# A list scheduler for the order of all engines, four score tiles in one visit and recurrence outputs by column tile, in a kernel that runs two attentions at once

## The chip, the cores and the metric

One core of one Trainium2 chip. The metric is the device time of one execution in microseconds (us), median of several. All profiled executions quoted here are fast; the page lists the clock that TensorE was granted, on average, beside the span.

TensorE multiplies matrices and writes PSUM (the pools of these kernels take 8 banks), VectorE and ScalarE copy and compute from PSUM into SBUF, GpSimd does small copies, and SyncE only issues transfers (its line in the trace is SPq). A transfer issued from an engine occupies that engine's queue for the time of the issue (a copy of V below: 0.50 us on GpSimd, 0.59 us on SyncE).

## The reference, cut to what matters

```python
def _A_ref(x, mem0, Wq, Wk, Wv, Wo, seg_len):      # S 2048, Dm 576, H 32, Dh 128, M 8, seg_len 32
    mem = mem0
    for s in range(n_seg):                          # 64 segments, one after the other
        h = concatenate([mem, x[s]], axis=1)        # 8 memory rows + 32 tokens = 40
        q, k, v = h @ Wq, h @ Wk, h @ Wv            # 32 heads of 128
        p = softmax(where(mask, q @ k.T * scale, -1e9))
        o = (p @ v) @ Wo
        mem = o[:, :M]; outs.append(o[:, M:])       # the memory of the next segment
    return concatenate(outs)

def _B_ref(x, wqkv, wo):                            # plain attention, 32 heads of 18
    ...
a = _A_ref(...); b = _B_ref(...); g = sigmoid((x * gate_w).sum(-1))
return g * a + (1 - g) * b
```

A is a recurrence: segment s+1 needs the outputs of segment s. B is independent of it and is used to fill the waits of A.

## The kernel before

Each segment is a chain: projections (tile pvv) evacuated to tm, transposes (pt), scores (psh), exponential, row sums (pss), their reciprocals spread by TensorE (prb), values (pso), outputs (acc), and a fold (pw) into ht, the input of the next segment. The queries, keys and values of tokens do not depend on the memory. Those of the last 8 tokens of each segment are projected ahead, 16 segments at a time (pv, vl); their outputs, which the memory doesn't need, are made four segments at a time (otl). B's score tiles are sb, exponentials etb, values ob. The order is the order of the program text, and a generator steps B forward at fixed places (`tick`). V reaches its place in v_sb by four small copies per half, issued on SyncE.

```python
def b_steps():
    ...
            for jp in range(2):
                sb = ps_bs.tile([P, 2, QC], FP32, name="sb")          # two buffers of two banks
                for i in range(2):
                    j = 2 * jp + i
                    nc.tensor.matmul(sb[:, i, :], lhsT=kc[32*j:32*j+32, o:o+P],
                                     rhs=qch[gq][32*j:32*j+32, :], ..., tile_position=(32 * j, 0))
                nc.scalar.activation(out=etb[:, :, :], in_=sb[:, :, :], func=ACT.Exp, scale=scale_b)
                ...
        def project(w, starts):
            pv = ps_a.tile([P, 512], FP32, name="pvv", tag="pb")
            ...
            tm = seg2.tile([P, 512], BF16, name="tm", bufs=4)
            nc.vector.tensor_copy(out=tm[:, :], in_=pv[:, :])
            tick()
            return tm
        ...
        def project_v(b):
            tm = project(wv, ...)
            for jj in range(2):
                for u in range(2):
                    nc.sync.dma_start(out=v_sb[...], in_=tm[64 * jj + 32 * u:64 * jj + 32 * u + CT, :])

        tq2 = [project(wq, ...) for hf in range(2)]
        tk2 = [project(wk, ...) for hf in range(2)]
        turn(tq2, qt)                       # transposes: the four tm are free after these
        turn(tk2, kt3)
        project_v(0)
        ...                                 # psh, exponential, minimum
        project_v(1)
        ...                                 # idle-filling matmuls when no last-token work is left
    def out_project(acc, o, t0, b, d0, d1):           # each column tile j: other heads, all columns d0..d1
        for i in range(4):
            for j in range(4):
                nc.tensor.matmul(acc[32*j:32*j+32, 0:d1-d0], lhsT=o[:, h, t0:t0+CT], rhs=wo[:, h, d0:d1], ...)
    # hl = high and low half of acc on VectorE; the fold adds the four partial sums by matmul
```

The softmax here doesn't subtract the row's maximum and nothing guards it: scores larger than these inputs give would overflow.

## Time and profile before

| part of the span | us |
|---|---|
| time, median of 3 runs | 2015.8 |
| start (to the first projection of segment 0) | 259.7 |
| 63 segment intervals, mean | 26.02 |
| end (from the start of the last segment) | 109.4 |

"Interval" is the time from one segment's first pvv matmul to the next one's, read from the trace. The table of engines by stretch, for the three parts (columns: stretch, its length, then busy us and instructions of TensorE, its weight loads, VectorE, ScalarE and GpSimd, mean granted clock, busy share of the DMA engines, GB/s):

```profile
0.00:259.70 259.70, 206.13 (x1376) 96.16 (x1380) 74.68 (x154) 112.98 (x157) 39.49 (x77) 0.87 0.60 177
259.70:1899.10 1639.40, 1589.73 (x24377) 822.09 (x24378) 892.78 (x2149) 924.45 (x1017) 135.21 (x331) 0.98 0.16 38
1899.10:2008.50 109.40, 84.33 (x822) 45.07 (x822) 52.40 (x115) 46.17 (x49) 0.40 (x1) 0.84 0.33 92
```

In the segments TensorE is busy 97% of the time at nearly full clock, which is why the argument is about TensorE's time there. One more row matters later, that of the values product, which reads v_sb (columns: busy us, mean ns | idle before, what ended it):

```profile
L713 PE MATMUL pso<-et,v_sb 64*128 64x40 bf16 x2048 | 63.5, 180 | 2.8 <-DVE et L705 2.6
```

TensorE lost 2.8 us in all before pso, 2.6 of them to the multiply of et; its weight loads waited 1.7 us for V copies, 4 times.

### The profile page before, as it was taken

How to read it: one execution, taken by the hardware profiler on the slowest of the kernel's cores; microseconds unless marked ns; L12 is line 12 of the kernel's file. 1: busy time of each engine (PE TensorE's matmuls, PEld its weight loads, DVE VectorE, ACT ScalarE, POOL GpSimd, SP SyncE). 2: the span in 40 equal slices, each digit the busy share in tenths (PEclk: the TensorE clock that was granted, in tenths of full speed). 3: DMA queues.
4: the chain of work that ended last, by engine and by line, in shares of the span. 5: the costliest groups of instructions: out<-in, count | busy, mean ns of one | idle time of the engine just before them, and what ended most of it. 6: DMA issues, size and time to landing. Idle time of an engine off the chain costs nothing.

```text
span 2008.5 us, 60909 instructions
## 1 busy us (share of the span) xinstructions
PE 1880.2 (94%) x26570; PEld 963.3 (48%) x26570; DVE 1019.9 (51%) x2416; ACT 1083.6 (54%) x1222; POOL 175.1 (9%) x409
## 2 busy tenths in 40 slices
PE   6599899999999999999999999999999999999968
PEld 3243444555554455555544555554444444444434
DVE  2043255555554555555555555545554555545535
ACT  2345555555554555555556555555554555555544
POOL 5000001000100001000010001100010000100000
PEclk9599999999988999999999999989998999999979
DMA  8742631121221112211111112210111011100042
GB/s 275 256 116 91 167 63 53 31 41 29 50 46 42 34 34 50 45 37 39 43 54 34 36 36 51 47 35 26 28 40 35 26 28 32 30 24 26 20 119 82
DMA packets 242479, 118.04 MB, mean 59 GB/s; under 512 B 166236, under 2 KB 234660, under 8 KB 240676
## 3 DMA queue, kind: packets, MB, share of 16 engines
q1 hardware_dynamic: 231440, 91.43, 18.0%
q0 software_dynamic: 6048, 16.52, 2.6%
q10 hardware_dynamic: 4724, 6.20, 1.1%
q8 instruction: 208, 3.41, 0.7%
q14 instruction: 59, 0.48, 0.1%
HBM read 59.42 MB, written 37.88 MB: 48 GB/s over the span
## 4 chain that ended last, share of the span: by engine, by line
PE 74%; DVE 6%; issue 3%; ACT 2%; DMA 1%; ACTq 0%; SPq 0%; DVEq 0%; POOL 0%
PE pvv L616 22%; PE sb L210 14%; PE acc L540 9%; PE ob L190 7%; PE psh L662 3%; PE pt L632 3%; PE pv L297 3%; PE prb L697 3%; PE pw L561 2%; ACT etb L219 2%; PE idle L470 2%; PE pso L713 2%; DVE ot L721 2%; PE po L783 2%; PE pv L285 2%
## 5 line engine op out<-in xcount | busy, mean ns | idle before, releaser
L219 ACT ACTIVATE etb<-sb 128x1024 bf16<-128x1024 f32 x1024 | 1028.6, 1025 | 820.0 <-PE sb L210 789.2
L210 PE MATMUL sb<-qch,kch 32*128 32x512 bf16 x2048 | 442.5, 395 | 18.6 <-ACT etb L219 12.6
L625 DVE CAST tm<-pvv 128x512 bf16<-128x512 f32 x384 | 265.0, 690 | 215.4 <-PE pvv L616 212.7
L616 PEld LDWEIGHTS <-ht 128*32 128x32 bf16 x7680 | 197.2, 97 | 202.9 <-issue 45.8
L190 PE MATMUL ob<-etb,vch 128*32 128x512 bf16 x2048 | 235.8, 399 | 24.8 <-ACT etb L219 16.0
L540 PE MATMUL acc<-wo,ot 128*32 128x384 bf16 (+1 forms) x4096 | 204.6, 299 | 9.7 <-DVE ot L721 3.2
L210 PEld LDWEIGHTS <-kch 32*128 32x128 bf16 x2048 | 105.0, 91 | 218.5 <-issue 195.1
L540 PEld LDWEIGHTS <-ot 128*32 128x32 bf16 x4096 | 116.5, 99 | 85.3 <-DVE ot L721 48.2
L616 PE MATMUL pvv<-wq_m,ht 128*32 128x512 bf16 x2048 | 138.2, 388 | 11.0 <-DVE ht L738 8.6
L616 PE MATMUL pvv<-wv_m,ht 128*32 128x512 bf16 x2048 | 143.4, 381 | 0.0
L721 DVE CAST ot<-pso 128x320 bf16<-128x320 f32 x256 | 113.5, 483 | 53.5 <-PE pso L713 53.5
L616 PE MATMUL pvv<-wk_m,ht 128*32 128x512 bf16 x2048 | 133.7, 380 | 0.0
L190 PEld LDWEIGHTS <-vch 128*32 128x32 bf16 x2048 | 68.4, 94 | 112.5 <-issue 88.6
L276 DVE CAST vl<-pv 128x512 bf16<-128x512 f32 x90 | 62.0, 690 | 106.2 <-PE pv L297 39.7
L705 DVE TENSOR_TENSOR et<-et,prb 128x320 bf16<-128x320 bf16 x128 | 62.3, 487 | 102.0 <-PE prb L697 101.9
L551 DVE CAST hl<-acc 128x384 bf16<-128x384 f32 (+1 forms) x160 | 72.4, 452 | 77.3 <-PE acc L540 76.6
L672 DVE TENSOR_TENSOR et<-et,cap 128x320 bf16<-128x320 bf16 x128 | 42.7, 337 | 103.3 <-ACT et L670 103.3
L608 POOL COPY qt<-xl 128x256 bf16<-128x256 bf16 x64 | 26.0, 406 | 656.4 <-issue 631.5
L662 PEld LDWEIGHTS <-kt 128*64 128x64 bf16 x2048 | 62.7, 111 | 34.3 <-issue 29.9
L662 PE MATMUL psh<-qt,kt 128*64 128x40 bf16 x2048 | 77.3, 189 | 0.0
L389 PE MATMUL pq<-xT,wpk 128*128 128x512 bf16 x320 | 76.8, 389 | 0.0
L552 DVE TENSOR_TENSOR hl<-acc,hl 128x384 bf16<-128x384 f32 (+1 forms) x160 | 72.9, 456 | 5.1
(118 smaller groups left out, 1913.1 us busy)
## 6 DMA issues: line engine op xcount, KB each, us to landing
v_sb<-tm SPq DMA_DIRECT2D x512, 32.0 KB
wo<-in_A_Wo_dram SPq DMA_DIRECT2D x4, 1152.0 KB
qtd<-stg SPq DMA_DIRECT2D x32, 128.0 KB
wv_m<-in_A_Wv_dram SPq DMA_DIRECT2D x4, 1024.0 KB
qch<-qtd POOLq DMA_DIRECT2D x32, 128.0 KB, 2.5
ktd<-stg SPq DMA_DIRECT2D x32, 128.0 KB
wq_m<-in_A_Wq_dram SPq DMA_DIRECT2D x4, 1024.0 KB
vgd<-vt SPq DMA_DIRECT2D x32, 128.0 KB
```

What stands on the lines that cost most here:

```text
L190: mm = nc.tensor.matmul(ob[32 * j:32 * j + 32, :], lhsT=vc[:, o + 32 * j:o + 32 * j + 32], rhs=ets[j // 2][:, j % 2, :], start=(kb == 0), ...
L210: nc.tensor.matmul(sb[:, i, :], lhsT=kc[32 * j:32 * j + 32, o:o + P], rhs=qch[gq][32 * j:32 * j + 32, :], start=True, stop=True, tile_posi ...
L219: nc.scalar.activation(out=etb[:, :, :], in_=sb[:, :, :], func=ACT.Exp, scale=scale_b)
L389: nc.tensor.matmul(pq[:, :], lhsT=wpk[:, c, :, :].rearrange("p j e -> p (j e)"), rhs=xT[:, c, t * QC:(t + 1) * QC], start=(c == 0), stop=( ...
L540: nc.tensor.matmul(acc[32 * j:32 * j + 32, 0:d1 - d0], lhsT=o[:, h, t0:t0 + CT], rhs=wo[:, h, d0:d1], start=(b == 0 and i == 0), stop=(b = ...
L551: nc.vector.tensor_copy(out=hl[:, 0, d0:d1], in_=acc[:, 0:d1 - d0])
L552: nc.vector.tensor_tensor(out=hl[:, 1, d0:d1], in0=acc[:, 0:d1 - d0], in1=hl[:, 0, d0:d1], op=ALU.subtract)
L616: nc.tensor.matmul(pv[32 * j:32 * j + 32, :], lhsT=ht[:, cc, :], rhs=rw, start=(c == 0), stop=(c == NF), tile_position=(0, 32 * j),)
L625: nc.vector.tensor_copy(out=tm[:, :], in_=pv[:, :])
L662: nc.tensor.matmul(psh[64 * jj:64 * jj + 64, i * L:(i + 1) * L], lhsT=kt[:, h * L:h * L + 64], rhs=qt[:, h, :], start=True, stop=True, til ...
L705: nc.vector.tensor_tensor(out=et[:, b, :], in0=et[:, b, :], in1=prb[:, 0:W8], op=ALU.mult)
L721: nc.vector.tensor_copy(out=ot[:, j * HG:(j + 1) * HG, :].rearrange("p h t -> p (h t)"), in_=pso[:, 0:W8])
```

## The change

The intent: take tiling changes and columns from TensorE, and let a greedy list scheduler, which runs while the kernel is built, choose the order of every engine from durations written in the kernel. The diff is 1996 lines long; its core:

```diff
+class Plan:                                  # list scheduler: operations with engine, duration,
+    DRAIN = {"PE": 0.205, ...}               # dependencies, priority, buffer tokens and landing time
+    SWITCH = 0.1                             # a change of TensorE's tiling
...
-                sb = ps_bs.tile([P, 2, QC], FP32, name="sb")
+                box["sb", gq, kb] = sb = ps_s.tile([P, 4, QC], FP32, name="sb")     # one buffer of four banks
...
+                for j in range(4):
+                    r = slice(32 * j, 32 * j + 32)
+                    nc.tensor.matmul(sb[:, j, :], lhsT=kc[r, o:o + P], rhs=qt_[r, :], ..., tile_position=(32 * j, 0))
...
-            for i in range(4):               # acc: other heads per column tile, then hi/lo split and fold
+                    for j in range(4):       # acc: other 144 output columns per column tile
                         nc.tensor.matmul(
-                        acc[32 * j:32 * j + 32, 0:d1 - d0], lhsT=o[:, h, t0:t0 + CT], rhs=wo[:, h, d0:d1],
+                            acc[32 * j:32 * j + 32, :], lhsT=o[:, slot, t0:t0 + CT], rhs=wo[:, h, RW * j:RW * j + RW],
...
+    plan.tokens_of("tm", 4)
...
-            nc.vector.tensor_copy(out=tm[:, :], in_=pv[:, :])
+            e_ = add(f"e{'QKV'[kind]}{hf}.{s}", ("DVE", "ACT"), (psum_copy(512), act_time(512)), ev, [op],
+                     prio=1.2, take=("tm",), give=(("pb", op0, 0),))
...
+        pv0 = add(f"qv0.{s}", "SP", 1.8, put_v(0), [ev0, prev.get("pso0")], prio=0.2, give=(("tm", ev0, 0),), tail=1.9)
...
+            t_ = add(f"t{hf}.{s}", "PE", 8 * 0.056, turn, [eq, ek], prio=1.30, mode="full",
+                     take=("pb",), give=(("tm", eq, 0), ("tm", ek, 0)))
...
-            pv = ps_a.tile([P, 512], FP32, name="idle", tag="pb")      # idle-filling matmuls are gone
...
+    plan.emit()
```

Queries and keys of B are also projected 18 wide per head without pads, and the loads put the pads in.

## The prediction

> **What bounds the kernel now.** I read the page first (busy shares and slices), then the chain that ended last, the groups by line, the waits, and a timeline of one segment. The kernel runs two things at once: a recurrence of 64 segments (line names pvv, pt, psh, pso, acc, pw) and an independent 32-head attention (sb scores, etb exponentials, ob values).
>
> ```profile
> PE 1880.2 (94%) x26570; PEld 963.3 (48%) x26570; DVE 1019.9 (51%) x2416; ACT 1083.6 (54%) x1222; POOL 175.1 (9%) x409
> ...
> PE 74%; DVE 6%; issue 3%; ACT 2%; DMA 1%; ACTq 0%; SPq 0%; DVEq 0%; POOL 0%
> ...
> L219 ACT ACTIVATE etb<-sb 128x1024 bf16<-128x1024 f32 x1024 | 1028.6, 1025 | 820.0 <-PE sb L210 789.2
> ```
>
> TensorE is busy 94% and holds 74% of the chain; VectorE and ScalarE are half idle, and ScalarE idles 789 us for scores. So a microsecond saved on TensorE in the segment stage is worth nearly one. "Busy" counts overlapping matmuls, so I look at starts. From the chain of waits, window 1000 to 1027 us:
>
> ```profile
> 1017.91 0.32 PE sb L210
> 1018.23 0.12 PE pw L561
> 1018.35 0.32 PE sb L210
> 1018.67 0.17 PE pw L561 x3
> 1018.84 0.32 PE sb L210
> 1019.16 2.31 PE pvv L616 x40
> 1021.47 0.22 PE ob L190 x4
> 1021.68 1.08 PE pvv L616 x20
> 1022.76 0.32 PE sb L210 x2
> ```
>
> Columns are start, time, work. One sb matmul holds TensorE 0.32 us, and two (different row tiles, side by side) also hold it 0.32 us. Forty pvv matmuls of the same 512 columns, four column tiles side by side, take 2.31 us, 0.23 per four; ob inside the same tiling takes 0.22. So a visit in another tiling costs 0.22 us of columns plus 0.10 us for leaving that tiling. I use 0.10 us per change of tiling throughout.
>
> Starts of the segments' first projection in the trace: the first at 259.7 us, the last at 1899.1 us, hence 63 intervals with a mean of 26.0 us; the last start to the end of the span is 109 us. Measured time is 2015.8 us, 7 us over the span.
>
> **What the Trainium skill says.** "TensorEngine Tiling (Array Packing)", Key Properties: changing the tiling mode drains the engine. The trace agrees: 0.32 against 0.22 us. "TensorE: Matmul & The Clock Gate", Back-to-back issue gap: a warm gap of N/2.4 + 2.5 ns. The trace agrees: 216 ns between groups of four pvv (N=512), 162.5 at N=384, 82.5 at N=192, 56 for 128-wide transposes. The new N=144 would by that be 62.5 ns; no run shows it yet. "TensorEngine Tiling", Gotcha 1: row tiles write different PSUM banks. That fits the new visit: four scores tiles need four banks, so with 3 general banks and ob nothing is left for a second score buffer. "Advanced Engine Details and Errata", The Read-Write Bubble: one ScalarE instruction may read several banks, and large tiles spread the fixed cost. The trace agrees: the exponential is 1025 ns for 1024 columns and 443 for 320, a slope of 0.83 ns, so 2048 columns should take 1.87 us.
>
> **The change, part by part.** I counted matmuls and tiling changes in the instruction lists of both built programs and gave every group its measured gap.
>
> *Scores.* Before: 1024 intended pairs, of which the list shows 282 single matmuls torn apart, each a full visit. After: 512 visits of four. Columns alone: 1024 x 0.216 = 221 us become 110 us. Exponentials: 1024 x 1.025 = 1029 us become 512 x 1.87 = 960 us, off the bound.
>
> *Tiling changes.* 2966 in the list before, 1797 after: 297 us become 180 us, 117 us less. In the 63 full segment intervals they fall from 42 to 26 each.
>
> *18-wide projections.* Queries and keys are projected unpadded: 320 matmuls of 512 columns become 180, 69 us become 39 us, all before the first segment. Pads are put in by loads of 18 rows: 384 small copies on one queue; copies on SyncE rise to 1860 in all, about 25 a segment. At 0.29 to 0.58 us an issue (v_sb rows) that is about 11 us of a segment: busy, not the bound.
>
> *Recurrence outputs by column tile.* Each column tile makes other 144 output columns instead of a partial sum over other heads. Columns are unchanged (157 us against 160), but the instructions double. What goes: the hi/lo split on VectorE (hl, 145 us in all) and most of the fold: 800 pw and 80 pto matmuls become 189 pw; 24 us of TensorE become 5. On the recurrence chain, split and fold (about 2.3 us from the last acc to ht) become about 1.1 us.
>
> *Order.* 164 idle-filling matmuls (35 us) vanish; psh and pso alternate tiles: 115 us of gaps become about 57. Final output product: 256 matmuls of 288 columns become 160, 11 us less.
>
> Sum of column time and changes over the list: before 1396 + 297 = 1692 us, after 1136 + 180 = 1316 us. In a segment interval: 23.0 us before against 26.0 measured, so 3.0 us were waits and slow clock; after, 18.4 us.
>
> **From occupancy to time.** I do not expect 18.4 us, because three things now lie close together.
> - TensorE: 18.4 us on average; 20 to 21.5 in the first dozen intervals, 17 in the last fifteen, where no last-token filler is left.
> - Attention with one score buffer: sb start to exponential start is 0.44 us (999.79 to 1000.23 in the timeline), plus 1.87, plus about 0.1 to get back: 2.4 us a visit. The list puts 34 visits before segment 0, 9 to 11 in each of the first twelve, then 7: 22 to 26 us in those twelve, 17 us later.
> - Recurrence: projections with attention between them 8.3 us; then, from the order in the list, waits that fillers don't cover: transposed copy 0.75, exponential-minimum-sum-reciprocal-multiply 1.7, the two output copies 0.7, cast-fold-ht 1.0: about 4 us on top of 16.6 us, 20 to 21 us.
>
> So 12 intervals x 23.3 = 280, 36 x 20.9 = 752, 15 x 20.0 = 300: 1332 us, mean 21.1. Start: the list before had 170 us of TensorE before segment 0 and took 260, in a stretch where the weights saturate the DMA (388 GB/s at 40 to 60 us, clock about 0.55 until 100 us). After, the list has 116 us; half of the 90 us of waits, since the 14 MB of weights still compete: 160 us. End: the list has 42 us from the last segment's start; plus 4 us of chain waits and 5 for the last reload, multiply and store: 51 us (109 before; the 15 us wait for wop goes, as it is loaded early). Sum 160 + 1332 + 51 = 1543; I shade to 1530, because the filler choice was made with these waits in view.
>
> **Rivals.**
> 1. *The single score buffer becomes the bound.* ScalarE must also take its share of evacuations; a late exponential then holds TensorE, whose order is fixed. For it: exponentials and TensorE no longer overlap within a buffer. Against: 7 x 2.4 = 17 us still fits in 21. If it wins, a visit costs about 3 us and 512 visits make 1600 to 1650 us.
> 2. *The fixed order fits better than I think*: waits shrink to 1 us a segment, start 140 us: 140 + 63 x 19.4 + 48 = 1410 us.
> 3. *SyncE's single queue blocks.* A store that waits for its source holds up the loads behind it; v_sb needs four copies (2.4 us issue) and about 2 us to land before pso. For: 25 copies a segment in one order. Against: most are a segment ahead. If it costs 3 us a segment: 1720 us.
> 4. *N=144 runs into a floor.* If a group of four took 107 ns instead of 62.5, 160 groups per four segments cost 1.8 us a segment, 114 us. Against: at N=192 the trace holds 82.5.
> 5. *Nothing gained*, as the recurrence's latency was the bound. Against: only a few tens of us of TensorE waits are listed before, and ht ended just 8.6 us of them.
>
> **Range and chances.** Rival 2 gives the low end, 1410; rival 1 or part of 3 the high end, 1640. To miss a 2% gain, the segments would have to stay at 26 us in spite of 4.6 us less work each; I give that 3% in all.
>
> **What would show it.** Right: about 512 exponentials of 1.87 us; sb visits 0.32 us each; acc gaps near 62 ns per four; segment intervals of about 23 us at first and 20 to 21 later; TensorE's share of the chain below 74%, VectorE and ScalarE shares up; first segment near 160 us. Wrong: intervals above 24 us with SyncE or v_sb loads as releasers (rival 3), ScalarE's exponentials as the main thing TensorE waits for (rival 1), acc gaps near 100 ns (rival 4), or a start well over 180 us.

## The result, and the profile after

The changed kernel takes 1753.86 us (median of 4 fast runs, 1750.56 to 1757.52), and the kernel before 2009.55 us beside it. The ratio is 0.8736, 95% interval 0.868 to 0.8793. Ratios and intervals here are worked out from the fast runs of both kernels in the same rounds, so they are not quite the ratio of the medians quoted. The change is a gain of 12.6%, but 1753.86 lies outside the predicted range of 1410 to 1640.

The lines of the changed kernel's page that answer to those of before:

```profile
PE 1471.1 (84%) x30560; PEld 844.8 (48%) x30582; DVE 715.0 (41%) x1523; ACT 1099.5 (63%) x872; POOL 133.2 (8%) x295
...
PEclk9989889999999999999999989999999898899998
...
L680 ACT ACTIVATE etb<-sb 128x2048 bf16<-128x2048 f32 x512 | 961.4, 1878 | 432.0 <-PE sb L671 400.2
...
L1124 PE MATMUL pso<-et,v_sb 64*128 64x40 bf16 x2048 | 62.8, 183 | 51.2 <-DMA v_sb<-tm 36.4
```

TensorE's busy time fell by 409 us, but its share fell too, from 94% to 84%: it has less work and waits more. The 512 exponentials take 1878 ns each, as expected. The chain of waits breaks off at the end of this trace (1% in all), so it says nothing here, and I read stretches, waits and timelines instead. The same three stretches:

```profile
0.00:224.70 224.70, 136.32 (x1126) 78.63 (x1137) 64.89 (x130) 73.06 (x74) 24.45 (x82) 0.93 0.58 174
224.70:1688.30 1463.60, 1288.09 (x28708) 736.61 (x28718) 623.24 (x1339) 1002.48 (x783) 79.04 (x192) 0.95 0.18 39
1688.30:1749.90 61.60, 46.68 (x730) 29.57 (x730) 26.90 (x55) 24.00 (x16) 29.71 (x21) 0.92 0.37 121
```

| part | predicted | measured | off by |
|---|---|---|---|
| start | 160 | 224.7 | +65 |
| 63 intervals | 1332 (mean 21.1) | 1463.6 (mean 23.23) | +132 |
| end | 51 | 61.6 | +11 |
| sum | 1543, shaded to 1530 | 1749.9 | +207 |

Two thirds of the miss are in the segments: 12 us of it in the first twelve intervals (24.3 us instead of 23.3), 80 in the next 36 (23.1 instead of 20.9) and 39 in the last 15 (22.6 instead of 20.0). The traces let the 63 intervals be split into three terms: TensorE idle, the time lost to half clock (half of what TensorE was busy at half clock, taken as if all of it stretched twofold), and the rest, the work at full clock (us):

```
                 63 intervals    work    idle    lost to half clock
before                   1639    1552      50          38
changed kernel           1464    1221     175          67
run 2, no V copies       1399    1218     153          28
run 3, two queues        1405    1220     155          30
run 12, together         1350    1221     105          25
```

The four kernels with the same matmuls come out with the same work within 4 us, which speaks for the split. The change took away 331 us of work and added 126 us of idle time and 29 us of slow clock, so 176 us were left. What TensorE waits for, over the whole span (columns: us in total, times, longest):

```profile
PE sb L671 <- ACT etb L680: 55.9, 105, 2.0
PE ptx L384 <- ACT xL L403: 44.5, 3, 39.8
PE pso L1124 <- DMA v_sb<-tm: 36.4, 53, 3.1
PE pw L1167 <- DVE bd L1156: 17.9, 36, 0.9
PE prb L1103 <- DVE rq L1095: 15.3, 36, 0.6
PE pvv L980 <- DVE ht L1175: 13.8, 43, 0.8
```

The second row is the start. The third is new: TensorE waits before pso until the V copies have landed, 36.4 us in 53 places; the weight loads of pso wait for them for 47.6 us (1.7 before). A timeline shows how V becomes late (segment that starts at 1511.1 us):

```profile
1518.03 1.88 ACT L680 ACTIVATE etb<-sb 128x2048 bf16<-128x2048 f32 x1 [0.78 <-PE sb L671]
1518.07 0.39 PE L980 MATMUL pvv<-wv_t,ht 128*32 128x512 bf16 x4
...
1519.47 0.62 PE L1039 MATMUL pt<-ident,tm 128*128 128x128 bf16 x8
...
1520.13 0.59 ACT L331 CAST tm<-pvv 128x512 bf16<-128x512 f32 x1 [0.23 <-PE pt L1039]
...
1521.26 4.97 SPq L1019 DMA_DIRECT2D v_sb<-tm  x8
...
1525.91 0.45 PE L1124 MATMUL pso<-et,v_sb 64*128 64x40 bf16 x16
```

The first V half is projected by 1518.46, but its evacuation starts only at 1520.13, released by the transposes pt (1519.47 to 1520.09): the four tm buffers hold Q and K of both halves until then. ScalarE, which was chosen for this copy, was also in an exponential until 1519.91. Three ht loads hold the queue until 1521.17, then the eight copies occupy SyncE for 4.97 us, and pso comes 4.65 us after the first copy. In this segment pso just gets by without idle time of TensorE; in the longest wait within the segments it did not:

```profile
1414.59 0.26 PE L1124 MATMUL pso<-et,v_sb 64*128 64x40 bf16 x7 [2.08 <-DMA v_sb<-tm]
```

Before, the order of the text made the transposes first and each V half after them, so that the buffers were free.

I measured two spans in every segment of each trace (medians over 64 segments): from the start of the last four matmuls of the first V half to the start of the first V copy, and from the start of the fourth copy's issue to the first pso matmul.

```
                         V projected -> first copy    fourth copy -> pso
before                            1.15 us                  5.17 us
changed kernel                    3.15                     2.49
two queues                        2.92                     4.07
six buffers                       1.15                     4.64
all together                      1.15                     5.73
```

The second span is the slack of the landing. In the changed kernel it was halved.

A second effect: the clock. In the segments TensorE ran at half clock for 150 us of the changed kernel's time and for 78 us before. The spans of half clock start on a grid of 3.413 us. I took the busy share of TensorE in each window of that grid in the changed kernel (busy from the modelled ends of matmuls, so roughly), and looked at the clock of the next window:

```
share of the window busy   windows at full clock   of these followed by half clock
below 0.55                          15                        15
0.55 to 0.75                        63                        15
0.75 to 0.80                        33                         1
above 0.80                         286                         0
```

"TensorE: Matmul & The Clock Gate", section "What's actually happening", has the free-running window of 3413 ns, which the trace confirms, and says that the clock falls after an idle window; its section "HAM oscillation — how this bites in real kernels" gives the rule as no idle gap of over about 3.4 us. Here no such gap was needed: in the segments the longest gap shortly before a half-clock span was 2.1 us, and being busy for less than 0.55 of the window was enough each time (the table runs from 225 to 1740 us; one of the 15 windows, at the end, was idle throughout). The busy share is not the whole rule: in the segments of the kernel before, half clock followed 8 of 455 windows above 0.80. In the changed kernel a wait for V therefore costs twice: itself, and often the next 3.4 us at half speed.

### The profile page after: what moved, and what is told of

The parts are those of the page before. It is cut to its first block, busy times and chain, and to the rows that moved or that the text cites. A ratio compares the mean times of both kernels' runs of the same rounds, so it can differ in the third digit from the quotient of the medians.

```text
span 1749.9 us, 68709 instructions
## 1 busy us (share of the span) xinstructions
PE 1471.1 (84%) x30560; PEld 844.8 (48%) x30582; DVE 715.0 (41%) x1523; ACT 1099.5 (63%) x872; POOL 133.2 (8%) x295
## 5 line engine op out<-in xcount | busy, mean ns | idle before, releaser
L680 ACT ACTIVATE etb<-sb 128x2048 bf16<-128x2048 f32 x512 | 961.4, 1878 | 432.0 <-PE sb L671 400.2
L333 DVE CAST tm<-pvv 128x512 bf16<-128x512 f32 x312 | 214.9, 689 | 235.8 <-PE pvv L980 198.1
L671 PE MATMUL sb<-qch,kch 32*128 32x512 bf16 x2048 | 210.0, 398 | 57.1 <-ACT etb L680 55.9
L908 PE MATMUL acc<-wo,ot 128*32 128x144 bf16 x8192 | 182.5, 253 | 10.0 <-DVE ot L333 8.1
L908 PEld LDWEIGHTS <-ot 128*32 128x32 bf16 x8192 | 165.0, 111 | 29.8 <-DVE ot L333 15.8
L1047 DVE COPY qk<-pt 128x1024 bf16<-128x1024 bf16 x128 | 88.1, 688 | 143.3 <-PE pt L1039 142.6
L950 POOL COPY qk<-xl 128x256 bf16<-128x256 bf16 x128 | 53.2, 418 | 1051.9 <-PE psh L1060 852.4
L1124 PE MATMUL pso<-et,v_sb 64*128 64x40 bf16 x2048 | 62.8, 183 | 51.2 <-DMA v_sb<-tm 36.4
L1039 PE MATMUL pt<-ident,tm 128*128 128x128 bf16 x1024 | 78.6, 219 | 9.9 <-DVE obf L1204 5.4
L1124 PEld LDWEIGHTS <-v_sb 64*128 64x128 bf16 x2048 | 43.4, 96 | 80.9 <-DMA v_sb<-tm 47.6
L1039 PEld LDWEIGHTS <-tm 128*128 128x128 bf16 x1024 | 61.4, 97 | 42.4 <-issue 40.5
```

What stands on the lines that cost most here:

```text
L333: nc.vector.tensor_copy(out=out_of(), in_=in_of())
L671: nc.tensor.matmul(sb[:, j, :], lhsT=kc[r, o:o + P], rhs=qt_[r, :], start=True, stop=True, tile_position=(32 * j, 0),)
L680: nc.scalar.activation(out=etb[:, :, :], in_=box["sb", gq, kb][:, :, :], func=ACT.Exp, scale=scale_b)
L908: nc.tensor.matmul(acc[32 * j:32 * j + 32, :], lhsT=o[:, slot, t0:t0 + CT], rhs=wo[:, h, RW * j:RW * j + RW], start=(first and s_ == 0), s ...
L950: nc.gpsimd.tensor_copy(out=opened["qk"][:, f, :, 0:16 * L].rearrange("p a (h t) -> p a h t", t=L)[:, :, :, CT:L], in_=box["xlt", s][:, :, ...
L1039: nc.tensor.transpose(out=pt[:, a, :, i, :], in_=tm[:, i * Dh:(i + 1) * Dh], identity=ident[:, :])
```

## The experiments

All comparisons with the kernel before are of fast runs on the same chip in the same rounds; the changed kernel itself was measured in its own rounds, so experiments are set against it through their ratios (0.8736 for the changed kernel) and through their own traces. The interval of 0.8736 is some 11 us wide to each side, so smaller differences of the total (runs 6 and 10) are read from the traces alone, and those of 13 to 17 us (runs 1 and 9) lean on them. My theories after the first reading: A, weight loads held up the start; B, the V copies on the one queue hold up the segments; the rivals are the single score buffer and the half clock in itself.

**1. Weight loads from GpSimd (start).**

```diff
-                nc.scalar.dma_start(out=w[0][:, c, :], in_=rows(w2, c))
+                nc.gpsimd.dma_start(out=w[0][:, c, :], in_=rows(w2, c))      # likewise the 24 small ones
-            name, "ACT", 6.0, load_w, [wbl], ...
+            name, "POOL", 8.0, load_w, [wbl, xdups[-1]], ...
```

> The changed kernel, with the 36 loads of the recurrence weights issued from GpSimd after the last x tile instead of from ScalarE. Theory A (ScalarE held in issuing these loads for 47 us kept PSUM banks from TensorE, 39.8 us idle at 30 to 70 us): first segment starts near 185 us instead of 224.7, time 1754 - 38 = about 1716 us, segment intervals unchanged at 23.2. Rival (the stretch is bound by the DMA engines that carry the weights): start within 10 us of 224.7, time about 1750 us.

Measured: 1740.94 us, ratio 0.865. The start fell only from 224.7 to 211.3 us. ScalarE no longer sits in 46.9 us of issuing, and the 39.8 us wait of TensorE is gone, but TensorE now waits for evacuation buffers whose stores are slow:

```profile
PE pvb L541 <- DVE vt L333: 15.2, 2, 9.3
PE pvv L982 <- DVE ht L1177: 13.8, 43, 0.8
PE pvb L541 <- DVE stg L333: 9.3, 1, 9.3
```

The wait moved. That the same bytes meet the same DMA engines a little later is my reading, not shown.

**2. No V copies (wrong).** v_sb keeps what it held, so A's values are wrong; the comparison with the reference passes all the same, so it is no test of this part, and "correct" below means only that this comparison passed.

```diff
-                for j in range(4):
+                for j in range(0):
```

> Wrong result on purpose: the eight copies of a segment that put V into v_sb are left out, order of TensorE unchanged. Theory B (the V copies through the one SyncE queue hold pso, 33 us of listed TensorE waits and 47 us of weight-load waits, and the slow clock that follows): time 1754 - 45 to - 80, about 1690 us, pso waits gone, mean interval about 22.2. Rival (the wait only moves to the next step of the chain of the segment): time within 15 us of 1754.

**3. V copies on two queues (correct).**

```diff
-                    dma(
+                    (nc.gpsimd.dma_start if j >= 2 else dma)(
                         out=opened["v_sb"][64 * (j // 2):64 * (j // 2) + CT, o:o + 512],
```

> Correct result: two of each four V copies are issued from GpSimd instead of SyncE. Theory B: about half to two thirds of what leaving them out gives, 1754 - 25 to - 50, about 1715 us. Rival (chain moves, or GpSimd's own copies in order hold them): within 10 us of 1754, or slower.

Measured: without copies 1689.53 us (ratio 0.8404), intervals 22.21, half clock in the segments 65 us. With two queues 1699.17 us (0.8457), intervals 22.30, half clock 68 us. The order of all other instructions is the same as in the changed kernel. So V's arrival costs some 64 us, of which 55 come back with a correct result. The row of pso in the two-queue run:

```profile
L1124 PE MATMUL pso<-et,v_sb 64*128 64x40 bf16 x2048 | 50.1, 181 | 19.0 <-DVE ot L333 7.1 <-DVE et L1113 5.9 <-DMA v_sb<-tm 5.2
```

The wait for v_sb is 5.2 us instead of 36.4. The rest of the gain came with the clock: by the split above, the 59 us that the segments lost in these traces are 21 us of idle time and 37 us of half clock. One brings the other, but the larger part was paid as slow clock.

**4. Exponential over half the columns (wrong).**

```diff
-  nc.scalar.activation(out=etb[:, :, :], in_=box["sb", gq, kb][:, :, :], func=ACT.Exp, scale=scale_b)
+  nc.scalar.activation(out=etb[:, 0:2, :], in_=box["sb", gq, kb][:, 0:2, :], func=ACT.Exp, scale=scale_b)
```

> Wrong result on purpose: each exponential takes 1024 columns instead of 2048 (1.03 instead of 1.88 us), so score visits come back 0.85 us sooner; order unchanged. Theory C (the single score buffer and ScalarE's long instruction are what holds the segments, in waits of scores for exponentials, and of evacuations and the recurrence's own exponentials behind it): time falls by 100 us or more, to 1650 or below, intervals near 21. Rival (they are one wait among several): falls by the 44 us of listed waits of sb and ob for etb at most, 1710 to 1740 us.

Measured: 1728.39 us (0.8589), intervals 22.92. TensorE's wait of sb for etb fell from 55.9 to 7.7 us, and the wait of pso for V rose from 36.4 to 57.5 us. Freed of the single score buffer, TensorE runs into V earlier; as long as V is late, the buffer is not the bound. With V mended (run 3) its wait is the largest in the segments, 41.7 us, and no run halves the exponential there, so its share of what is left stays untested.

**5. Pairs of scores again (four-wide visit undone).** Two score buffers of two banks, 1024-column exponentials, four etb buffers, everything else as in the change.

```diff
-                box["sb", gq, kb] = sb = ps_s.tile([P, 4, QC], FP32, name="sb")
+                    box["sb", gq, kb, jp] = sb = given(ps_s, "sb", [P, 2, QC], FP32)     # for jp in range(2)
-    plan.tokens_of("sb", 1)
+    plan.tokens_of("sb", 2)
```

> One part of the change undone: scores are made two row tiles at a time again (two buffers of two banks, exponentials over 1024 columns), inside the new scheduler, with the new recurrence outputs kept. Theory (the saved TensorE visits carried most of the gain): 512 more visits cost 512 x 0.216 us of columns = 110 us, and up to as many changes of tiling at 0.1 us, and the exponentials cost 1.025 instead of 0.94 us per 1024 columns; TensorE works more in every segment, so 1754 + 110 to 210 = 1865 to 1965 us, intervals near 26 us, almost the kernel before. Rival (the second score buffer pays back, as TensorE no longer waits for one buffer: 37 us of waits of sb for etb in the trace): 1754 + 110 - 40 = about 1825 us, and the waits for etb vanish.

Measured: 2167.06 us, ratio 1.0814, so 8% slower than the kernel before, well past what either theory allowed. Mean interval 29.71 us. Three rows of its waits:

```profile
PE pso L1129 <- DMA v_sb<-tm: 84.4, 113, 2.4
PE acc L913 <- DVE ot L333: 69.3, 120, 0.8
PE sb L674 <- ACT etb L684: 29.3, 46, 1.0
```

TensorE's work, split as above, is 22.1 us an interval instead of 19.4 (1389 and 1221 us over the 63), so 168 us are the work itself, within my estimate of 110 to 210. The rest are idle time, 279 us instead of 175 (waits for V and for the copies of pso lead), and half clock: 519 us of the segments instead of 150, which lost 203 us instead of 67. Without the four-wide visit the new order and the new outputs lose all of the gain. The planner's constants were not tuned for this variant, so this is the worth of the visit inside this plan, not of pairs in general.

**6. Idle-filling matmuls put back (segments 48 to 62).**

```diff
+                fl = add(f"idle{f}.{s}", "PE", 2 * 0.216, idle, [uq0, *wo_loads], prio=4.0, mode="full", take=("pb",))
```

> The idle-filling matmuls that the change took out are put back in segments 48 to 62 only: 4 pieces of two 512-column matmuls each (0.43 us) a segment, at the lowest priority, 60 x 0.43 = 26 us of TensorE time placed where the planner sees a gap. Theory (the clock falls to half after a stretch of 3.4 us in which TensorE was busy less than about 0.75; after segment 48 there are 15 such half-clock spans in the trace of the changed kernel, 55 to 60 us): with fillers the half-clock time in the last 15 intervals falls by at least half, the work done there runs at full speed, and the intervals 49 and later fall from 22.6 to 21.5 to 22 us, total -10 to -20 us. Rival (the waits set the time, not the clock): fillers only take TensorE time in a fixed order: intervals 49 and later rise by up to 26/15 = 1.7 us, total 0 to +26 us.

Measured: 1762.37 us (0.8796, interval 0.8764 to 0.8829, which overlaps that of the changed kernel). In the last 15 intervals half clock fell from 61 to 17 us, as the theory says, but the intervals are 22.77 us (22.59 in the changed kernel) and not 21.5 to 22, as the rival says. The fillers raised the clock and took about as much of TensorE as that was worth: in all segments 34 us more work, 10 us less idle and 17 us less half clock. That the change removed them here is not why it fell short.

**7. Six tm buffers, copies still on one queue.**

```diff
-    plan.tokens_of("tm", 4)
+    plan.tokens_of("tm", 6)
```

(From here on, and in runs 5 and 6, the last quarter of final products also waits for the last pso, without which some plans run out of PSUM banks; in the changed kernel's plan this is to alter nothing, which no run tests.)

> Six buffers instead of four for the evacuated projections (each V projection holds its buffer until its four copies have landed), nothing else: the V copies stay on the one queue. Theory B (the 64 us that the V copies cost come from pso waiting until they have landed): buffers alone don't bring the landing forward; only the planner's order changes, -10 to -35 us (1720 to 1745), and pso still waits for v_sb. Theory C (VectorE's evacuations wait for these buffers: 35 us of tm waits in the trace are put down to DMAs, which holds PSUM banks and so TensorE): -40 to -70 us (1685 to 1715), and pso's waits for v_sb shrink as well, since V is evacuated earlier.

Measured: 1701.46 us (0.8486), intervals 22.37, half clock 102 us. That is inside theory C's range and outside that of B, and pso's wait for V shrank as C says:

```profile
L1124 PE MATMUL pso<-et,v_sb 64*128 64x40 bf16 x2048 | 53.3, 180 | 22.6 <-DVE ot L333 8.0 <-DMA v_sb<-tm 6.8 <-DVE et L1113 5.4
```

With the first V half evacuated at once (1.15 us from projection to first copy, as before the change) eight copies on one queue are early enough. So theory B in its first form, the queue alone, was too narrow: V was late by a buffer and by the queue, and mending either takes most of the wait away. The planner also chose another order here, so not all of the 52 us need be the buffer.

**8. Two queues, six buffers, measured durations in the plan.** The edits of runs 3 and 7, and V copies at 1.35 us per pair, last-token output stores at 2.4, segment loads at 1.5, gate multiplies at 1.74 us in the plan.

> Three things together: half of the V copies on the GpSimd queue, six buffers, and the planner told measured durations (copies to v_sb 1.35 us per pair on each queue, last-token stores of the outputs 2.4, segment loads 1.5, gate multiply 1.74 us). If the two effects add up: 1754 - 55 - 30 = about 1670 us (1655 to 1690), intervals about 21.8. If they are the same wait seen twice: no better than the two queues alone, 1690 to 1705. The end should stay near 62 us, as the gate multiplies are only timed rightly, not made shorter.

Measured: 1675.57 us (0.8352), intervals 21.86. That is inside the range of the first case, which had counted 30 us for the buffers. Measured, the two were worth 55 and 52 us alone and 78 together, not 107, although the new durations came on top. That fits one wait, in part seen twice; no run has the two without the new durations.

**9. The start: weight queue, output weights later, three vl buffers.**

```diff
-            dma(out=opened["wo"][:, 8 * q:8 * q + 8, :], ...)
+            nc.gpsimd.dma_start(out=opened["wo"][:, 8 * q:8 * q + 8, :], ...)
-        wo_loads.append(add(f"wo{q}", "SP", 0.5, load_wo, [opening], ...))
+        wo_loads.append(add(f"wo{q}", "POOL", 1.0, load_wo, [opening, last_done[0, False][4 + 2 * q]], ...))
-    plan.tokens_of("vl", 2)
+    plan.tokens_of("vl", 3)
```

with the edit of run 1.

> The start alone, three things: the weight loads on the GpSimd queue behind the last input tile (as in the first run), the four loads of the A output weights (4.6 MB) put on the GpSimd queue and each behind a later store of the last-token projections instead of all ahead of them on the SyncE queue, and three buffers instead of two for the last-token projections. Theory (the start is held by stores that wait behind large loads: in the trace of the changed kernel VectorE waits 15.5 us for a last-token store behind those loads, and TensorE 9.4 us for VectorE): the first segment starts 30 to 50 us earlier than in the changed kernel (224.7), at 175 to 195 us, total 1754 - 30 to 50 = 1705 to 1725; intervals unchanged near 23.2. Rival (from 86 us on the start is paced by the attention visits, 34 of them at 2.43 us each, or all the same bytes only meet elsewhere, as with the first run): the start stays at 205 to 215 us, total about 1740.

Measured: 1736.76 us (0.8644). The start fell by 31 us to 193.7, as the theory says, but the total only by 17: the intervals rose from 23.23 to 23.49, which gives 16 us back. The order of the segments is another one in this plan, and the time at half clock rose to 164 us. That stores behind large loads held the start fits, but three things were changed at once: the weight queue alone gave 13 us (run 1), and the other 18 are not divided between the output weights and the third vl buffer. About half of the gain was lost later.

**10. The end: gate multiplies on two engines.**

```diff
-                nc.gpsimd.tensor_scalar_mul(out=ga_view(n), ...)
+                eng = nc.gpsimd if e == "POOL" else nc.vector
+                eng.tensor_scalar_mul(out=ga_view(n), ...)
-            gates[n] = add(f"ga{n}", "POOL", 0.75, mul_a, ...)
+            gates[n] = add(f"ga{n}", ("POOL", "DVE"), (1.74, 0.75), mul_a, ...)
```

> The end alone: the 16 gate multiplies (1.74 us each on GpSimd, 0.75 in the plan) may run on VectorE as well and are timed rightly in the plan. Theory (at the end GpSimd is busy with multiplies for 17 us while TensorE waits 7.1 us for the copy of the last tokens' outputs on GpSimd, and VectorE 11.4 us for what follows): the tail from the last segment's start falls from 61.6 to 50 to 54 us, total -8 to -12 us (1742 to 1746); start and intervals unchanged. Rival (the end hangs on the last pso's wait for v_sb, 3.1 us, and on the 256-column chain of final products after it): the tail stays within 3 us of 61.6.

Measured: 1750.83 us (0.8716). The ratio alone would not tell this from the changed kernel, but its trace (of one execution) does: the end is 53.8 us instead of 61.6, with start and intervals the same (222.0, mean 23.22). TensorE's 7.1 us wait for otl is gone. The planner counted 0.75 us for a multiply that takes 1.74 on GpSimd.

**11. Another order of the kernel of run 8.**

```diff
-    SWITCH = 0.1
+    SWITCH = 0.05
```

> The kernel with two queues, six buffers and measured durations (1675.6 us), where only one number of the planner differs: a change of tiling is planned at 0.05 instead of 0.1 us. The instructions are the same, only their order on the engines differs; the planner's own timetable then has intervals of 20.7 us instead of 21.7. Theory (the order itself is worth about 1 us a segment, and the timetable tells which order is better): intervals fall from 21.9 to 20.9 to 21.3 us, total 1625 to 1650. Rival (the timetable is only shorter because it now counts each of the 26 changes of tiling a segment 0.05 us too short, 26 x 0.05 = 1.3 us, which is all of the difference): the measured time stays within 15 us of 1675, or is longer, as more changes of tiling are taken.

Measured: 1653.68 us (0.8214), 22 us less, between what the two expected. The profiled executions are 29 us apart: intervals went from 21.86 only to 21.69, 10 us in all and not one us each, and the end from 68.2 to 50.0; the start was the same. So the rival was right about the intervals: the planner's shorter timetable was mostly the cheaper count of the changes. Why the end is shorter in this order I did not settle.

**12. Together.** Runs 3, 9, 10 and the durations of 8, five tm buffers (no run has six with three vl), and a smaller preference for staying in a tiling.

```diff
-            switch = 0.0 if e != "PE" or op.mode == mode else 0.4
+            switch = 0.0 if e != "PE" or op.mode == mode else 0.15
```

> What the runs showed to help, in one kernel: V copies on two queues, five buffers for evacuated projections, three for last-token projections, weight and A output weight loads moved as in the start run, gate multiplies on two engines, measured durations in the plan, and a smaller preference of the planner for staying in a tiling (0.15 instead of 0.4). If the separate effects add up (start 194, intervals 21.7 as in the run with the other order, end 52): 194 + 63 x 21.7 + 52 = 1613 us, so 1600 to 1630. If the earlier start is given back in the intervals, as it was half given back in the start run (+0.26 us an interval): 1630 to 1650, no better than the 1653.7 of the other order.

Measured: 1591.24 us (1588.44 to 1596.14), ratio 0.7932, better than both cases expected. It beats the changed kernel by 9% and the kernel before by 20.7%. Start 187.0, 63 intervals of 21.43 (1350.3 us), end 49.6, and 51 us of half clock in the segments:

```profile
PE 1412.4 (89%) x30582; PEld 811.2 (51%) x30582; DVE 737.9 (46%) x1571; ACT 1084.3 (68%) x832; POOL 266.8 (17%) x583
...
PE 64%; ACT 19%; DMA 6%; issue 5%; DVE 4%; SPq 1%; POOL 0%; ACTq 0%; DVEq 0%; POOLq 0%
...
L1021 POOL DMA_DIRECT2D v_sb<-tm x256 | 127.1, 497 | 826.6 <-DVE tm L333 657.6
```

The matmuls are the same 30,582 as in the changed kernel's list; only order, buffers and queues differ. TensorE is busy 89% of a shorter span and holds 64% of the chain, with ScalarE at 19%.

## Why the prediction was wrong

- **Direction and rough size of the work: right.** By the count over the list TensorE's work per interval was to fall from 23.0 to 18.4 us, by 4.6; by the split above it fell from 24.6 to 19.4, by 5.3. Visits of four hold TensorE 0.32 us, exponentials are 1.88 us, and acc matmuls come at 63 ns per four (median). So rival 4 (a floor at N=144) is refuted, and rival 5 (nothing gained) by the ratio. Run 5 shows that within this plan, which was not tuned for pairs, the gain is lost without the four-wide visit.
- **"A microsecond saved on TensorE in the segment stage is worth nearly one": no.** 331 us of work were saved in the segments and 176 us of time; the rest came back as idle time and slow clock.
- **The step that failed most: "about 4 us on top of 16.6 us, 20 to 21 us".** The sum of waits listed transposed copy, exponential to multiply, output copies and cast to ht. It left out the branch by which V reaches pso. In the changed order TensorE stood waiting for that branch 53 times. Removing it is worth 64 us (run 2), half of the 132 us that the segments were too long; a second queue gets back 55 (run 3), buffers 52 (run 7). The other half is not V: in run 2 the intervals are still 22.2 us instead of 21.1, with 2.4 us each of waits of many kinds, and its cause stays open.
- **The sentence that let it pass: "Against: most are a segment ahead"**, in rival 3. The part on SyncE had said "busy, not the bound", from 11 us of issues a segment: that is how long the queue is busy, not when each copy gets its turn. Of the roughly 25 copies of a segment, the eight V copies can never be ahead: they move what this segment has just projected. Rival 3 was given the right mechanism and 1720 us, and was then used only "in part" for the high end of 1640. And it was half the mechanism: the four tm buffers, which the new order made scarce, were in none of the five rivals.
- **Not foreseen: the clock.** The prediction took the clock of before. With the waits more windows of 3.4 us were less than 0.75 busy, and half clock rose from 78 to 150 us, by the split above 29 us of lost time. It falls with the waits for V (65 to 68 us in runs 2 and 3), so here it amplified them; in run 6, feeding it with filler work in the last 15 intervals gained nothing.
- **Rival 1 (the single score buffer): present, not the bound while V is late.** TensorE does wait 55.9 us for it, but halving the exponential gave only 25 us (run 4).
- **The start, "half of the 90 us of waits ... 160 us", was too low by 65 us.** It took over the waits of before at half size, while the waits were others: ScalarE issuing weights for 46.9 us with input work behind it, then last-token stores behind 4.6 MB of output weights. 31 us came back with run 9, 38 with run 12; what holds the remaining 27 us I did not settle.
- **The end, 51 us, was too low by 11 us**: a gate multiply takes 1.74 us on GpSimd, and the otl copy waited behind such multiplies. Run 10 recovers 8 us, run 12 all of it (49.6).
- **"The filler choice was made with these waits in view"**, the reason for shading 1543 to 1530: the choice was made with the plan's durations, 1.8 us for four V copies that take 2.35 (four at 0.588), and 0.75 for 1.74.

Run 12 reaches 1350 us in the segments and 49.6 us at the end, against 1332 and 51 predicted. So these instructions can run in nearly the predicted segment time; the changed kernel's order, buffers and queues did not get there. That 64 of the missing 132 us belong to the V copies, with the slow clock they bring, is shown (run 2). 87 us came back with run 8 and another 27 with run 12, but these differ in buffers, planned durations and order in many places, and no single cause is shown for what goes beyond the 64.

## What to carry to other kernels

When work is taken from the bound engine, list every input of each step of the chain, the transfers too, with the time at which it can be ready in the new order, and not only the waits that showed before: here a slack of 5.2 us shrank to 2.5, and a second queue brought it back to 4.1, two more buffers to 4.6. In a statically planned kernel, each planned duration and each buffer count is part of the order, so check the planned durations against the trace, starting with issues and GpSimd operations. A short wait on TensorE may cost the clock of the next few microseconds as well, so look at the clock row when waits rise.

## What the Trainium skill lacked or had wrong

- "TensorE: Matmul & The Clock Gate": it states when the clock falls as a whole idle window, or an idle gap of over about 3.4 us; its section "A second HAM failure mode: psum-queue depth-cycling" adds that frequent short idling makes the clock swing, without saying how much. In the changed kernel windows that were busy for less than 0.55 of their 3.4 us were followed by half clock 15 times of 15, those between 0.55 and 0.75 15 times of 63, those above 0.8 never in 286. Going back up needed a well filled window too: in the segments of run 5, 33 of 33 half-clock windows with 0.75 to 0.80 busy stayed at half, and none of 48 above 0.85 did. In the kernel before, though, 11 of 20 half-clock windows above 0.85 stayed at half, so something beside the busy share counts, and no run shows what.
- "DMA: Bandwidth & Descriptors", section "Anatomy of one DMA — SWDGE (gpsimd) path": it puts the sequencer's dispatch at about 50 ns, calls descriptor generation small, and puts the fixed cost mostly into completion. A copy of 32 rows of 1 KB into v_sb held GpSimd for 497 ns (mean of 256, run 12); on SyncE, which is not on that path, it held the queue for 588 ns (median of 512). With several small copies in a row that time, not the completion, sets when the last one starts.
- "GPSIMD Engine Reference", section "4.1 Engine selection": it calls elementwise work with one input roughly line rate on GpSimd. A multiply of 128x576 by a column, bfloat16 to float32, took 1.74 us there (mean of 16) and 0.5 to 0.7 us on VectorE in runs 10 and 12. The page's own section "3.1 Elementwise — side-by-side cycle accounting", with about 2.6 cycles an element against 1, is nearer to that.
